# Fourier mixing and a gated feed-forward on one core: column blocks of 512, 512 and 481, with the left 66 tokens of each batch collected in one buffer

## The chip, the core and the metric

The kernel runs on one core of a Trainium2 chip. The engines that matter here are TensorE (PE, matrix multiply; its weight loads are listed as PEld), VectorE (DVE), ScalarE (ACT), GpSimd (POOL) and SyncE (SP), whose queue issues most of the DMAs. Each engine runs its own instructions in order and waits for others by semaphores. The DMAs of all queues run on the core's 16 DMA engines. The metric is the time of one execution on the device, in microseconds (us); lower is better.

## The reference

The input x has 8 batches of 3008 tokens with 256 channels. The reference takes the real part of a two-dimensional Fourier transform over tokens and channels, and sends every token through a feed-forward layer with a ReLU gate.

```python
X = np.fft.fft(x, axis=1)
X = np.fft.fft(X, axis=2)
x = X.real.astype(np.float32).reshape(B * S, D)      # B, S, D = 8, 3008, 256
gate = np.maximum(x @ w_gate, 0.0)                   # w_gate: 256 x 1536
val = x @ w_val
out = (gate * val @ w_out).astype(np.float32)        # w_out: 1536 x 256
```

## The kernel before, in words

**The transform.** The transform of a real signal is symmetric, so the output token k and its mirror S-k are made of the same two parts, a cosine part and a sine part, once added and once subtracted. The kernel folds the input of a batch (POOL, `fold_steps`, lines 102 to 151), multiplies the folded rows with sine and cosine tables on PE (`dft_steps`, L385), and keeps the two parts of 1505 token columns in the tiles `U` and `V`. The channel transform is multiplied into the weights beforehand: `WA` and `WB` are applied to `U` and `V`, and `WM` is the matrix that turns a plus token into its mirror token (minus 2 times `WB`).

**Tiles.** The 1505 columns of a batch are cut into blocks: in batch 0 into four `segments` of 376 or 377, in batches 1 to 7 into three `thirds` of 504, 504 and 497. For every block the kernel goes over the NF = 12 chunks `fi` of 128 of the 1536 hidden channels. One such tile gives `h`, a bf16 tile of 128 hidden channels by two halves, plus and minus, of up to 512 columns each. The minus half is written in reverse order of columns.

**A slot** (`slot`, batches 1 to 7) is one round of the loop over tiles. PE's order in it is: the sine part of the next tile (L689, one matmul), some output steps, the cosine part of the next tile (L696, one matmul), the mirror matmul of the tile before (L575), the value of this tile (L570 and L571, two matmuls), and the rest of the output steps. DVE's order is: the minus product of the tile before (`second`, L597), the plus product of this tile (L597), and the sum for the next tile (`both`, L700). ACT copies the sine part out (L692) and writes a seed into a PSUM bank (`seed`, L684). POOL makes the second of two gates (L701) and, in batches 1 to 5, the folds of the batch after next in between (`run_fold`). Some tiles (every sixth in batch 1, every twelfth in batches 2 to 5) are of an older kind: three gate matmuls in place of the sine and cosine parts, and no L701. The DFT matmuls of the next batch are spread over the first two blocks of a batch, in groups of three (`DFT_EVEN`, `DFT_ODD`); each six of them are followed by two copies on ACT and two sums on DVE (`sums`, L397).

**Output steps** (`out_steps`). When a block's twelve `h` tiles are there, its output is made during the next block. A unit is 128 columns of one half: 12 matmuls (L496), one for each `h` tile, with `h` as the loaded weights and `wo` as the moving operand, 256 columns wide, which add up in a PSUM tile `o`. Two units share a PSUM tile; after them ACT copies it to a tile `os` (L502, four buffers), and SP stores the rows of each unit (L511), every second row of the output. A block of a batch 1 to 7 has eight units, so 96 steps; `per_tile = len(todo_out) // NF` is the number of steps in a slot, eight. A block's `chunks` list says which 128 columns a unit takes, and which rows of them are stored: 128, 120 or 121, once 127; columns at a border between the four segments belong to two units. After the last block, nothing is left to overlap, and its 96 steps run by themselves.

The order of instructions is fixed when the kernel is built; each engine keeps it.

The change touches `thirds`, `segments`, `first_row`, `out_steps`, `half_h`, `second`, `add_h`, `tile_of` and `per_tile`.

Of the kernel before, what the change touches and what calls it, by code (L numbers as in the profile page):

```python
# [11 lines left out]
BF16 = mybir.dt.bfloat16  # L12
# [15 lines left out]
def dram(ap, offset, pattern):  # L28
    return bass.AP(ap.tensor, offset, [list(p) for p in pattern])
# [3 lines left out]
def kernel(  # L33
# [27 lines left out]
    def single(name, shape, dt=F32, pool=const):  # L61
        return pool.tile(shape, dt, name=name, tag=name)
# [6 lines left out]
    wo = single("wo", [128, NF, D], BF16)  # L69
    hp = ctx.enter_context(tc.tile_pool(name="hp", bufs=2 * NF + 2, space=SB))  # L70

    wr = [[None] * 3 for i in range(2)]
    for c in range(3):
        for i in range(2):
            wr[i][c] = hp.tile([128, 2, 512], BF16, name="h", tag="h")
    XD = single("XD", [128, 2, 3, 2, D])
    XG = single("XG", [128, 2, 3, 2, D])
    PQ = single("PQ", [128, 2, 3, 2, D])
# [96 lines left out]
    def iota(dst, pattern, base, mult):  # L175
        nc.gpsimd.iota(dst, pattern=pattern, base=base, channel_multiplier=mult, allow_small_or_imprecise_dtypes=True)
# [41 lines left out]
            load_mirror(0, t, r)  # L218

    def load_w(i, c):  # L220
        nc.gpsimd.dma_start(out=wr[i][c][:], in_=(moe_w_gate, moe_w_val)[i][:, c * 512:(c + 1) * 512].rearrange("(c p) f -> p c f", p=128))
    for c in range(3):
        for i in range(2):
            load_w(i, c)
# [35 lines left out]
    for n, c in enumerate(order):  # L260
        q, m = (single(f"{s}{c}", [128, NJ], pool=st_) for s in "qm")
# [41 lines left out]
    for t in range(3):  # L303
        p, ts = slice(0, ROWS[1][t]), slice(t, t + 1)
# [154 lines left out]
    def new_uv():  # L459
# [2 lines left out]

    thirds = [
# [3 lines left out]
    ]  # L469
    segments = [(s * NJ, NJ, [(0, 0, 128, s, 0), (128, 0, 128, s, 128), (248, 8, 120, s, 256)], None) for s in range(3)]  # L470
    segments.append((3 * NJ, NE, [(0, 1, 127, 3, 0), (128, 0, 128, 3, 127), (249, 7, 121, 3, 255)], (0, 0)))

    def first_row(seg, j, plus):

        if seg == 0:
            return 2 * j + 1 if plus else S - 2 * j - 1
        if seg == 1:
            return H + 2 * j + 1 if plus else H - 2 * j - 1
        if seg == 2:
            return H + 2 * j if plus else H - 2 * j  # L480
        return 2 * j + 2 if plus else S - 2 * j - 2

    def out_steps(b, block, hs):
        c0, n, chunks, zero = block
        units = [(sign, ch) for sign in range(2) for ch in range(len(chunks))]
        steps = []
        for k in range(0, len(units), 2):
            st = {}
            for q in range(2):
                sign, ch = units[k + q]  # L490
                h0 = n - 128 - chunks[ch][0] if sign else chunks[ch][0]
                for f in range(NF):
                    def mm(st=st, q=q, f=f, sign=sign, h0=h0):
                        if "p" not in st:
                            st["p"] = psO.tile([128, 2, D], F32, name="o", tag="o")
                        nc.tensor.matmul(st["p"][:, q, :], lhsT=hs[f][:, sign, h0:h0 + 128], rhs=wo[:, f, :],  # L496
                                         start=(f == 0), stop=(f == NF - 1))
                    steps.append(mm)

            def fin(st=st, k=k):  # L500
                os_ = rp.tile([128, 2, D], F32, name="os", tag="os", bufs=4)
                nc.scalar.copy(os_[:], st["p"][:])  # L502
                for q in range(2):
                    sign, ch = units[k + q]
                    _, p0, cnt, seg, j = chunks[ch]
                    r0 = first_row(seg, j, sign == 0)
                    if seg == 2 and j == 0 and sign == 1:
                        p0, cnt, r0 = p0 + 1, cnt - 1, r0 - 2
                    if sign:
                        p0, r0 = 128 - p0 - cnt, r0 - 2 * (cnt - 1)  # L510
                    nc.sync.dma_start(out=dram(out, (b * S + r0) * D, [[2 * D, cnt], [1, D]]),  # L511
                                      in_=os_[p0:p0 + cnt, q, :])
                    if zero and zero[0] == ch and sign == 0:
                        nc.sync.dma_start(out=dram(out, b * S * D, [[D, 1], [1, D]]), in_=os_[zero[1]:zero[1] + 1, q, :])
# [28 lines left out]
    todo_out, todo_dft, todo_fold = [], [], []  # L543
# [42 lines left out]

    def half_h(st, sign):

        return st["h"][:, 1, st["n"] - 1::-1] if sign else st["h"][:, 0, 0:st["n"]]

    def mult(st, sign, r=None):
        n = st["n"]
        nc.vector.tensor_tensor(half_h(st, sign), (r or st["r"])[:, 0:n], st["v"][:, 0:n], op=ALU.mult)  # L593

    def relu_mult(st, sign):
        n = st["n"]
        nc.vector.scalar_tensor_tensor(half_h(st, sign), in0=st["s"][1 + sign][:, 0:n], scalar=0.0, in1=st["v"][:, 0:n],  # L597
                                       op0=ALU.max, op1=ALU.mult)

    def second(st):  # L600
        (relu_mult if "s" in st else mult)(st, 1)

    def finish(st):
        mirror(st["v"], st, 1)
        second(st)
# [8 lines left out]
        relu(st)  # L614

    def tile_of(block, fi, uvc):
        c0, n = block[:2]
        cols = slice(c0, c0 + n)
        return {"n": n, "fi": fi, "f": slice(fi * 128, (fi + 1) * 128), "us": uvc[0][:, cols], "vs": uvc[1][:, cols], "c": uvc[2][:, cols]}

    def add_h(st, hs):
        st["h"] = hp.tile([128, 2, 512], BF16, name="h", tag="h")
        hs.append(st["h"])

    def single_tile(st, outs, extra=(), last=(), tag="p"):
# [39 lines left out]
    def new_tiles():  # L665
        for b in range(1, B):
            for blk, block in enumerate(thirds):
                for fi in range(NF):
                    st = tile_of(block, fi, uv[b])
                    st["kind"] = "o" if b < 6 and fi % (6 if b < 2 else 12) == 5 else "n"  # L670
                    yield st

# [30 lines left out]
    def slot(cur, mid, nxt, after, outs, fold_us):  # L703
# [20 lines left out]
        if pending is not None:  # L724
            second(pending)
# [16 lines left out]

    uv = {0: (U, V, CB)}
    tiles, ahead = new_tiles(), []

    for b in range(B):
# [4 lines left out]
        for blk, block in enumerate(blocks):  # L751
            hs = []
# [8 lines left out]
            if blk == (0 if b else 2) and b + 1 < B:  # L761
# [94 lines left out]
```

## Time and profile before

| | before |
|---|---|
| time, median of 3 runs | 647.6 us (647.58 to 647.83) |
| span of the profiled execution, first to last instruction | 646.1 us |
| what lies around the span, median less span | 1.5 us |
| granted TensorE clock | 1.000 |
| busy in the span | PE 620.9, PEld 401.6, DVE 543.7, ACT 450.6, POOL 535.5 us |
| output matmuls (L496) | 2304, of 128x256 |
| stores of output rows on SP | 200 |

All lines that follow are of one profiled execution. In a row of the timeline the columns are: start, duration (both in us from the span's start), engine, line of the kernel, operation, the tile written and those read, shape and count; what stands in brackets is idle time of the engine before it, and who ended it. In a row of the windows table the columns are: the stretch, its length, then the busy time of PE, PEld, DVE, ACT and POOL with instruction counts, then the granted clock, the mean busy share of the 16 DMA engines, and GB/s. SPq is SP's queue: a DMA's row there is its issue. Matmuls overlap in the pipeline, so the distance from start to start of two matmuls, not the duration of one, says what it costs. The first two batches differ from the others in their staging; the steady part runs from about 115 us, the first block of batch 1, to 631 us, and the end, output only, from there.

### The profile page before, as it was taken

The numbers are of one execution on the slowest core, as the hardware profiler recorded it, in microseconds if no ns is written. First come the engines' busy times: TensorE is split into PE (matmuls) and PEld (weight loads), VectorE is DVE, ScalarE is ACT, GpSimd is POOL, SyncE is SP. The second block draws the span as 40 slices with busy tenths as digits, with TensorE's granted clock in tenths as the row PEclk, the third lists the DMA queues.
The fourth block names the chain that finished last, engine by engine and source line by source line (L and its number), as shares of the span: only waits on it lengthen the run. The fifth ranks groups of instructions, "written<-read, shape, count | busy, mean of one in ns | idle before, by whom it ended". The sixth has DMA issues, their size and how long they took to land.

```text
span 646.1 us, 12223 instructions
## 1 busy us (share of the span) xinstructions
PE 620.9 (96%) x4160; PEld 401.6 (62%) x4160; DVE 543.7 (84%) x970; ACT 450.6 (70%) x822; POOL 535.5 (83%) x593
## 2 busy tenths in 40 slices
PE   0999999999999999999999999999999999999996
PEld 0356676566666666666666666666666666666665
DVE  8875566887888899898998889988899899999990
ACT  8697666767666776777677677676777767777751
POOL 8589997899999999999899999999876656666660
PEclk9999999999999999999999999999999999999999
DMA  8922544224332433241222422311211111111112
GB/s 227 207 67 64 178 127 137 62 68 145 89 83 63 127 98 90 64 136 58 89 84 78 129 73 82 93 35 49 73 34 49 44 62 49 35 48 49 50 49 79
DMA packets 42438, 55.24 MB, mean 85 GB/s; under 512 B 5153, under 2 KB 32353, under 8 KB 42376
## 3 DMA queue, kind: packets, MB, share of 16 engines
q1 hardware_dynamic: 34552, 39.23, 19.7%
q0 software_dynamic: 7536, 14.72, 9.3%
q8 instruction: 32, 0.52, 0.4%
q10 hardware_dynamic: 288, 0.52, 0.2%
q14 instruction: 30, 0.25, 0.1%
HBM read 32.14 MB, written 24.67 MB: 88 GB/s over the span
## 4 chain that ended last, share of the span: by engine, by line
PE 69%; DVE 12%; POOL 9%; issue 6%; ACT 3%; DMA 0%; DVEq 0%; SPq 0%; ACTq 0%; POOLq 0%
PE o L496 27%; PE v L575 7%; PE v L570 7%; PE v L571 7%; DVE h L597 6%; PE g L689 5%; PE p L696 5%; DVE r L700 5%; POOL r L701 4%; PE d L385 4%; PE p L575 1%; POOL XG L113 1%; POOL PQ L121 1%; POOL XG L102 1%; PE p L571 1%
## 5 line engine op out<-in xcount | busy, mean ns | idle before, releaser
L701 POOL TENSOR_TENSOR r<-r 128x504 f32<-128x504 f32 (+1 forms) x234 | 291.7, 1252 | 73.8 <-DVE r L700 72.3
L496 PE MATMUL o<-wo,h 128*128 128x256 bf16 x2304 | 342.3, 273 | 0.0
L597 DVE SCALAR_TENSOR_TENSOR h<-r,v 128x504 bf16<-128x504 f32 (+1 forms) x468 | 297.3, 673 | 51.1 <-PE v L575 37.8
L496 PEld LDWEIGHTS <-h 128*128 128x128 bf16 x2304 | 225.2, 98 | 114.7 <-issue 2.3
L684 ACT ACTIVATE p<-CB,b 128x504 f32<-128x504 bf16 (+1 forms) x234 | 160.0, 684 | 55.3 <-DVE r L700 52.8
L692 ACT COPY r<-g 128x504 f32<-128x504 f32 (+1 forms) x234 | 135.0, 577 | 58.6 <-PE g L689 54.5
L700 DVE SCALAR_TENSOR_TENSOR r<-r,p 128x504 f32<-128x504 f32 (+1 forms) x234 | 156.7, 670 | 0.6 <-ACT r L692 0.6
L575 PE MATMUL v<-V,WM 128*128 128x504 bf16 (+3 forms) x296 | 108.6, 367 | 1.6 <-DVE h L597 1.0
L570 PE MATMUL v<-U,WA 128*128 128x504 bf16 (+3 forms) x296 | 108.6, 367 | 0.1
L571 PE MATMUL v<-V,WB 128*128 128x504 bf16 (+3 forms) x296 | 108.7, 367 | 0.0
L593 DVE TENSOR_TENSOR h<-r,v 128x376 bf16<-128x376 f32 (+3 forms) x124 | 68.9, 580 | 25.7 <-PE v L575 13.6
L689 PE MATMUL g<-V,WM 128*128 128x504 bf16 (+1 forms) x234 | 87.8, 375 | 0.5 <-ACT r L692 0.3
L696 PE MATMUL p<-U,WA 128*128 128x504 bf16 (+1 forms) x234 | 87.8, 375 | 0.0
L502 ACT COPY os<-o 128x512 f32<-128x512 f32 x96 | 55.7, 580 | 14.5 <-PE o L496 8.1
L570 PEld LDWEIGHTS <-WA 128*128 128x128 bf16 x366 | 35.7, 98 | 38.3 <-issue 8.9
L571 PEld LDWEIGHTS <-WB 128*128 128x128 bf16 x366 | 35.7, 98 | 35.7 <-ACT WB L291 0.7
L102 POOL DMA_INDIRECT XG<-in_x_dram,gidx x48 | 48.8, 1017 | 8.7 <-issue 6.3
L113 POOL TENSOR_TENSOR XG<-XG,XD 128x510 f32<-128x510 f32 x42 | 52.5, 1265 | 0.1
L585 ACT ACTIVATE r<-g 128x504 f32<-128x504 f32 (+3 forms) x48 | 27.3, 569 | 35.0 <-PE g L571 31.8
L585 ACT ACTIVATE r<-p 128x376 f32<-128x376 f32 (+1 forms) x80 | 38.2, 490 | 18.7 <-PE p L575 10.9
L121 POOL TENSOR_TENSOR PQ<-XG 128x510 f32<-128x510 f32 x42 | 45.0, 1091 | 0.0
L575 PEld LDWEIGHTS <-WM 128*128 128x128 bf16 x366 | 35.8, 98 | 11.4 <-issue 0.2
(127 smaller groups left out, 430.4 us busy)
## 6 DMA issues: line engine op xcount, KB each, us to landing
out_dram<-os SPq DMA_DIRECT2D x118, 128.0 KB
XD<-in_x_dram SPq DMA_DIRECT2D x30, 256.0 KB
out_dram<-os SPq DMA_DIRECT2D x62, 120.0 KB
XD<-in_x_dram SPq DMA_DIRECT2D x16, 240.0 KB
CB<-ch SPq DMA_DIRECT2D x7, 376.2 KB
out_dram<-os SPq DMA_DIRECT2D x10, 127.0 KB
XG<-in_x_dram,gidx POOLq DMA_INDIRECT x48
h<-in_moe_w_gate_dram POOLq DMA_DIRECT2D x3, 256.0 KB
```

The source lines that it names most:

```text
L496: nc.tensor.matmul(st["p"][:, q, :], lhsT=hs[f][:, sign, h0:h0 + 128], rhs=wo[:, f, :], start=(f == 0), stop=(f == NF - 1))
L570: nc.tensor.matmul(bank[:, 0:st["n"]], lhsT=WA[i][:, st["f"]], rhs=st["us"], start=True, stop=False)
L571: nc.tensor.matmul(bank[:, 0:st["n"]], lhsT=WB[i][:, st["f"]], rhs=st["vs"], start=False, stop=True)
L575: nc.tensor.matmul(bank[:, 0:st["n"]], lhsT=WM[i][:, st["f"]], rhs=st["vs"], start=False, stop=True, skip_group_check=True)
L593: nc.vector.tensor_tensor(half_h(st, sign), (r or st["r"])[:, 0:n], st["v"][:, 0:n], op=ALU.mult)
L597: nc.vector.scalar_tensor_tensor(half_h(st, sign), in0=st["s"][1 + sign][:, 0:n], scalar=0.0, in1=st["v"][:, 0:n], op0=ALU.max, op1=ALU.mult)
L684: nc.scalar.activation(st["p"][:, 0:st["n"]], st["c"], ACTF.Copy, scale=b2[:, st["fi"]:st["fi"] + 1])
L689: nc.tensor.matmul(st["g"][:, 0:n], lhsT=WM[0][:, st["f"]], rhs=st["vs"], start=True, stop=True)
L692: nc.scalar.copy(q[:, 0:n], st["g"][:, 0:n])
L696: nc.tensor.matmul(st["p"][:, 0:n], lhsT=WA[0][:, st["f"]], rhs=st["us"], start=False, stop=True, skip_group_check=True)
L700: nc.vector.scalar_tensor_tensor(sp[:, 0:n], in0=q[:, 0:n], scalar=-0.5, in1=st["p"][:, 0:n], op0=ALU.mult, op1=ALU.add)
L701: nc.gpsimd.tensor_tensor(sm[:, 0:n], sp[:, 0:n], q[:, 0:n], op=ALU.add)
```

## The change

The three blocks of a batch become 512, 512 and 481 columns wide. The two halves of an `h` tile now stand directly one behind the other, 2n columns, and a unit takes 128 of these 2n columns, across the border of the halves if it falls so. 512 columns make 2 x 512 / 128 = 8 whole units. 481 columns make 962 = 7 x 128 + 66: seven whole units, and 66 columns are left. After the minus product of each tile of such a block, a DMA on SP's queue copies these 66 columns of `h` to `LB`, a buffer of 12 x 256 columns that is filled as a ring over the batches (`keep_rest`). As soon as 128 columns are collected, the block's output gets one more unit that reads them from `LB`; in the last batch the 78 that remain make a unit of 78. `per_tile` is rounded up; blocks with 7 units have 84 steps, 7 in a slot. The segments of batch 0 keep six units each, the last of which overlaps the one before. The rows to store are worked out column by column (`row_of`), and a unit is stored in as many DMAs as it has runs of rows with a distance of two; a border between segments inside a unit cuts a run.

```diff
-            wr[i][c] = hp.tile([128, 2, 512], BF16, name="h", tag="h")
+            wr[i][c] = hp.tile([128, 1024], BF16, name="h", tag="h")[:].rearrange("p (c f) -> p c f", c=2)
...
-    thirds = [
-        (0, 504, [(0, 0, 128, 0, 0), (128, 0, 128, 0, 128), (256, 0, 120, 0, 256), (376, 0, 128, 1, 0)], None),
-        (504, 504, [(0, 0, 128, 1, 128), (128, 0, 120, 1, 256), (248, 0, 128, 2, 0), (376, 0, 128, 2, 128)], None),
-        (1008, 497, [(0, 0, 120, 2, 256), (121, 0, 128, 3, 0), (249, 0, 128, 3, 128), (369, 8, 120, 3, 256)], (0, 120)),
-    ]
+    thirds = [(0, 512), (512, 512), (1024, 481)]
+    segments = [(s * NJ, NJ) for s in range(3)] + [(3 * NJ, NE)]
+    REST = 33
+    LB = single("LB", [128, NF, 256], BF16)
+    left_rows, left_done = [], 0
...
     def out_steps(b, block, hs):
-        c0, n, chunks, zero = block
-        units = [(sign, ch) for sign in range(2) for ch in range(len(chunks))]
+        nonlocal left_done
+        c0, n = block
+        r = [row_of(c0 + i, True) for i in range(n)] + [row_of(c0 + n - 1 - i, False) for i in range(n)]
+        r = [None if v is None else b * S + v for v in r]
+        units, whole = [], n // 64
+        if n < 481:
+            whole = 6
+        for k in range(whole):
+            h0 = min(128 * k, 2 * n - 128)
+            units.append((lambda f, h0=h0: hs[f][:, h0:h0 + 128], [None] * (128 * k - h0) + r[128 * k:h0 + 128]))
+        if n == 481:
+            left_rows.extend(r[128 * whole:])
+            while len(left_rows) - left_done >= 128 or b == B - 1 and left_done < len(left_rows):
+                o = left_done
+                k = min(128, len(left_rows) - o)
+                units.append((lambda f, o=o, k=k: LB[:, f, o % 256:o % 256 + k], left_rows[o:o + k]))
+                left_done += k
...
-                        nc.tensor.matmul(st["p"][:, q, :], lhsT=hs[f][:, sign, h0:h0 + 128], rhs=wo[:, f, :],
+                        nc.tensor.matmul(st["p"][0:m, q, :], lhsT=lhs(f), rhs=wo[:, f, :],
                                          start=(f == 0), stop=(f == NF - 1))
...
+                if len(some[-1][1]) == 128:
+                    nc.scalar.copy(os_[:, 0:len(some)], st["p"][:, 0:len(some)])
+                for q, (_, r) in enumerate(some):
+                    if len(some[-1][1]) < 128:
+                        nc.scalar.copy(os_[0:len(r), q], st["p"][0:len(r), q])
+                    p = 0
+                    while p < len(r):
+                        e = p + 1
+                        while r[p] is not None and e < len(r) and r[e] == r[e - 1] + 2:
+                            e += 1
+                        if r[p] is not None:
+                            nc.sync.dma_start(out=dram(out, r[p] * D, [[2 * D, e - p], [1, D]]), in_=os_[p:e, q, :])
+                        p = e
...
     def half_h(st, sign):
-        return st["h"][:, 1, st["n"] - 1::-1] if sign else st["h"][:, 0, 0:st["n"]]
+        n = st["n"]
+        return st["h"][:, 2 * n - 1:n - 1:-1] if sign else st["h"][:, 0:n]
...
+    def keep_rest(st):
+        o, h0 = 2 * REST * (st["b"] - 1) % 256, 896
+        while h0 < 962:
+            k = min(962 - h0, 256 - o)
+            nc.sync.dma_start(out=LB[:, st["fi"], o:o + k], in_=st["h"][:, h0:h0 + k])
+            o, h0 = 0, h0 + k
...
     def second(st):
         (relu_mult if "s" in st else mult)(st, 1)
+        if st["n"] == 481:
+            keep_rest(st)
...
-            per_tile = len(todo_out) // NF
+            per_tile = -(-len(todo_out) // NF)
```

More of the change, by code (lines that the diff above doesn't have):

```diff
@@ L220, in load_w @@
     def load_w(i, c):
-        nc.gpsimd.dma_start(out=wr[i][c][:], in_=(moe_w_gate, moe_w_val)[i][:, c * 512:(c + 1) * 512].rearrange("(c p) f -> p c f", p=128))
+        nc.gpsimd.dma_start(out=wr[i][c], in_=(moe_w_gate, moe_w_val)[i][:, c * 512:(c + 1) * 512].rearrange("(c p) f -> p c f", p=128))
     for c in range(3):
@@ L460, in new_uv, with row_of @@
         return [up.tile([128, 4 * NJ + 2], BF16, name=n, tag=n) for n in ("U", "V")]
-    thirds = [
[3 rows of a table removed]
-    ]
-    segments = [(s * NJ, NJ, [(0, 0, 128, s, 0), (128, 0, 128, s, 128), (248, 8, 120, s, 256)], None) for s in range(3)]
-    segments.append((3 * NJ, NE, [(0, 1, 127, 3, 0), (128, 0, 128, 3, 127), (249, 7, 121, 3, 255)], (0, 0)))
-    def first_row(seg, j, plus):
+    thirds = [(0, 512), (512, 512), (1024, 481)]
[3 more added lines that the diff above has]
+    left_rows, left_done = [], 0
+    def row_of(col, plus):
+        seg, j = (3, col - 3 * NJ) if col >= 3 * NJ else divmod(col, NJ)
         if seg == 0:
@@ L479, in first_row @@
         if seg == 2:
-            return H + 2 * j if plus else H - 2 * j
-        return 2 * j + 2 if plus else S - 2 * j - 2
+            return H + 2 * j if plus else (H - 2 * j if j else None)
+        return 2 * j if plus else (S - 2 * j if j else None)
     def out_steps(b, block, hs):
-        c0, n, chunks, zero = block
-        units = [(sign, ch) for sign in range(2) for ch in range(len(chunks))]
+        nonlocal left_done
[15 more added lines that the diff above has]
+                left_done += k
         steps = []
@@ L488, in out_steps, with mm @@
             st = {}
-            for q in range(2):
-                sign, ch = units[k + q]
-                h0 = n - 128 - chunks[ch][0] if sign else chunks[ch][0]
+            some = units[k:k + 2]
+            for q, (lhs, r) in enumerate(some):
                 for f in range(NF):
-                    def mm(st=st, q=q, f=f, sign=sign, h0=h0):
+                    def mm(st=st, q=q, f=f, lhs=lhs, m=len(r)):
                         if "p" not in st:
                             st["p"] = psO.tile([128, 2, D], F32, name="o", tag="o")
-                        nc.tensor.matmul(st["p"][:, q, :], lhsT=hs[f][:, sign, h0:h0 + 128], rhs=wo[:, f, :],
+                        nc.tensor.matmul(st["p"][0:m, q, :], lhsT=lhs(f), rhs=wo[:, f, :],
@@ L497, in mm, with fin @@
                                          start=(f == 0), stop=(f == NF - 1))
                     steps.append(mm)
-            def fin(st=st, k=k):
+            def fin(st=st, some=some):
                 os_ = rp.tile([128, 2, D], F32, name="os", tag="os", bufs=4)
[L502 to L514, printed above, removed]
+                if len(some[-1][1]) == 128:
[11 more added lines that the diff above has]
+                        p = e
@@ L616, in tile_of @@
     def tile_of(block, fi, uvc):
-        c0, n = block[:2]
+        c0, n = block
         cols = slice(c0, c0 + n)
@@ L621, in add_h @@
     def add_h(st, hs):
-        st["h"] = hp.tile([128, 2, 512], BF16, name="h", tag="h")
+        st["h"] = hp.tile([128, 1024], BF16, name="h", tag="h")
         hs.append(st["h"])
@@ L669, in new_tiles @@
                     st = tile_of(block, fi, uv[b])
+                    st["b"] = b
                     st["kind"] = "o" if b < 6 and fi % (6 if b < 2 else 12) == 5 else "n"
```

## The prediction

> **What bounds the kernel now.** I read the page's busy times first, then the timeline of a slot in the steady part, then that of a slot with fewer output steps, then the DMA table by short windows around single stores and at the end. The page says that PE decides:
>
> ```profile
> span 646.1 us, 12223 instructions
> PE 620.9 (96%) x4160; PEld 401.6 (62%) x4160; DVE 543.7 (84%) x970; ACT 450.6 (70%) x822; POOL 535.5 (83%) x593
> ```
>
> The timeline shows a steady slot (batch 4, last block, 497 columns), from one `value` matmul of L571 to the next:
>
> ```profile
> 403.65 0.37 PE L571 MATMUL v<-V,WB 128*128 128x497 bf16 x1
> 403.71 1.26 DVE L597 SCALAR_TENSOR_TENSOR h<-r,v 128x497 bf16<-128x497 f32 x2 [0.15 <-PE v L575]
> ...
> 404.40 0.71 PE L496 MATMUL o<-wo,h 128*128 128x256 bf16 x5
> ...
> 405.57 0.37 PE L571 MATMUL v<-V,WB 128*128 128x497 bf16 x1
> ```
>
> 405.57 - 403.65 = 1.92 us. Matmuls overlap: their starts stand 0.109 us apart at 256 columns and 0.21 at 504, so five wide ones and eight output steps make 5 x 0.21 + 8 x 0.109 = 1.92: PE has no gap. At 504 columns the trace repeats 1.936. DVE needs three operations a slot; two of them take 1.26 of which the last lasts 0.67, so they follow each other every 0.59, and three need 1.77 of 1.94: the second bound is only 0.17 below. Where a slot has six output steps (batch 1, first block), that second bound shows:
>
> ```profile
> 116.01 0.38 PE L575 MATMUL v<-V,WM 128*128 128x504 bf16 x1
> ...
> 116.44 0.38 PE L571 MATMUL v<-V,WB 128*128 128x504 bf16 x1
> ...
> 116.50 1.27 DVE L597 SCALAR_TENSOR_TENSOR h<-r,v 128x504 bf16<-128x504 f32 x2 [0.55 <-PE v L575]
> ...
> 117.82 0.37 PE L575 MATMUL v<-V,WM 128*128 128x504 bf16 x1
> 117.82 0.10 PEld L570 LDWEIGHTS <-WA 128*128 128x128 bf16 x1 [0.20 <-issue]
> ...
> 118.24 0.37 PE L571 MATMUL v<-V,WB 128*128 128x504 bf16 x1
> ```
>
> PE would need 1.936 - 2 x 0.109 = 1.72; the slot takes 1.80, since the mirror matmul at 117.82 waits for the two DVE products (116.50 + 1.27 = 117.77), which waited for the mirror matmul before. That loop is a floor under every slot.
>
> The third thing is the stores. The page counts ten of 127 rows:
>
> ```profile
> out_dram<-os SPq DMA_DIRECT2D x10, 127.0 KB
> ```
>
> One is issued at 563.44. The windows after it, and those at the kernel's end (last two columns: busy share of the 16 DMA engines, GB/s):
>
> ```profile
> 567.00:568.00 1.00, 1.00 (x8) 0.63 (x7) 0.99 (x2) 0.58 (x1) 0.39 (x1) 1.00 0.07 26
> 568.00:569.00 1.00, 1.00 (x9) 0.70 (x8) 0.93 (x2) 0.97 (x2) 0.93 (x1) 1.00 0.07 25
> 569.00:570.00 1.00, 1.00 (x9) 0.62 (x7) 0.93 (x2) 0.74 (x3) 0.33 (x1) 1.00 0.07 24
> ```
>
> ```profile
> 642.00:643.00 1.00, 0.00 (x0) 0.00 (x0) 0.00 (x0) 0.42 (x1) 0.00 (x0) 1.00 0.00 0
> 643.00:644.00 1.00, 0.00 (x0) 0.00 (x0) 0.00 (x0) 0.00 (x0) 0.00 (x0) 1.00 0.55 169
> 644.00:645.00 1.00, 0.00 (x0) 0.00 (x0) 0.00 (x0) 0.00 (x0) 0.00 (x0) 1.00 0.29 85
> 645.00:646.00 1.00, 0.00 (x0) 0.00 (x0) 0.00 (x0) 0.00 (x0) 0.00 (x0) 0.91 0.00 0
> ```
>
> A share of 0.07 is one engine of 16: the 127 rows run one after the other at 24 to 26 GB/s, 42.5 ns for a row of 1 KB. By the completion events in the trace such a store lands 7.2 us after its issue at best (median of the ten 7.6), one of 128 rows in 1.7 to 1.8 and one of 120 in 1.9 to 2.0 at quiet times. Today's last two stores (128 and 120 rows, issued at 642.45 and 642.85) have landed at 644.83; the span ends 1.3 later.
>
> **PE's part.** Batches 1 to 7 make 24 output units each, 168; after, 23 each and 4 units of collected rows, 165. Three units x 12 matmuls = 36 fewer, which the instruction order confirms (72 PE rows less, a load and a matmul each). At 0.109 that is 3.9 us. They fall in three places, the first blocks of batches 2, 4 and 6, where per_tile goes from 8 to 7. Wider and narrower blocks cancel: 24 slots a batch gain 8 columns and 12 lose 16, at 5 matmuls x 0.42 ns (0.109 us for 256) both ways.
>
> Not all of the 3.9 arrives. A slot with 512 columns and 7 steps needs 1.936 + 8 x 5 x 0.42 ns - 0.109 = 1.84 on PE. The loop above grows by 8 columns in one matmul and two products, 8 x (0.42 + 1.0 + 1.0) ns = 0.02, to 1.83 (1.0 ns is DVE's step: 0.46 us back to back at 376 columns, 0.59 at 504). So the slot just fits, but the DFT's four sums a block (L397, every 0.26 us when back to back) lose their cover: 1.94 - 1.77 = 0.17 a slot today, 0.05 after. Batch 1's first block prices this: from its first L571 matmul at 114.24 to the next block's at 138.54 it takes 24.30. PE alone would take the 25.43 of batch 2's first block, less 24 x 0.109, plus one matmul of 0.21 for its second tile of the old kind: 23.03. Of the 1.27 over, eight slots x 0.08 = 0.7 is the floor, and 0.57 is sums. With 7 steps I take 0.5 a block, 1.5 in all; the bounds are 0 and 4 x 0.26 x 3 = 3.1. POOL adds a little: in batch 2's first block its result (L701) is ready only 0.03 and 0.5 us before DVE takes it at two tiles, and the block would be 1.1 shorter. Bounds 0 and 0.6, I take 0.2, as DVE's lead of some 0.4 covers most. Batch 1, already at the floor and behind POOL, gets wider tiles in 24 slots and loses 0 to 0.3; I take 0.1. Sum: 3.9 - 1.5 - 0.2 - 0.1 = 2.1 us gained.
>
> **The copies of the left 66 columns.** 96 DMAs (seven times 12, one batch split in two) of 128 x 132 B, put on SP's queue behind `second`, and 48 more stores; at 0.25 to 0.43 us of issue each some 50 us on a queue that spent 421 us waiting for `os L502`. Queued behind a copy are only stores: `os` has four buffers and is reused some 23 us later. The row loads for XD are issued in first blocks, where only tile 11's copy stands. The matmuls that read LB come 84 steps, over 9 us, after that copy's issue, also at the end, against about 2 us for a small store: cost 0; without that cover it would be 2 us once. 48 LB weight loads wait for a DMA; today's weight loads with a satisfied wait (L689 behind a DMA) start on the usual 0.109 beat, so 0. The product that overwrites a copied `h` comes 26 tiles, 50 us, later: 0.
>
> **The end.** Here the change costs. The row runs are cut at segment borders, and in the last block of a batch the stores have 104+24, 128, 128, 97+31, 128, 128, 89+38 rows, then the collected rows, in batch 7 12+66. In the trace the completion events of a store number 16 for 128 rows, 15 and one at once for 120, 11 and one for 121, one and one for 127 and for 1: the number of engines is the largest divisor of the row count up to 16. 97, 31 and 89 have none, so each runs on one engine, and by the trace on the same one: the 127 rows issued at 630.93 land at 638.13, and the four stores behind them (128, 120, 1 and 128 rows) are complete only after that, at 638.5 to 639.2, 3.9 to 7.2 us from their issue.
> The Trainium skill's page "DMA: Bandwidth & Descriptors", section "Why a DMA increments its semaphore by 16 and not by 1", states the same: the largest k up to 16 that divides the outer sizes, on the lowest-numbered engines. The counts above agree for 1, 120, 121, 127 and 128 rows; no run shows 97, 31 or 89. By that rule the sum is the one that follows; by the quiet 120-row stores the end would cost 0.4.
>
> The second pair of the last block is copied at 636.60 in today's frame, so its 97 rows are issued at about 637.6. From there the first engine has 97 + 31 + 8 + 8 + 89 + 19 (38 rows on two) + 1 + 6 (66 on eleven) = 259 rows x 42.5 ns = 11.0 us. A 127-row store has 7.2 - 5.4 = 1.8 besides its rows. 637.6 + 1.8 + 11.0 = 650.4, against 644.8: 5.6 late. The 1.8 holds some receipt that a chain may not repeat, so I take 5.4. Bounds: 0.4 if these stores spread (only two more issues of some 0.35 at the end, less one smaller copy), 6.3 if each single-engine store brings the 0.3 us hiccup that the packets of the one at 631 show. In mid-kernel the same stores are late by as much and nobody waits.
>
> **The sum.** Span 646.1 - 2.1 + 5.4 = 649.4. The median of the timed runs, 647.6, is 1.5 above this execution's span; so 650.9.
>
> **Rivals.** (a) Faster: the stores of 97, 31 and 89 rows spread over engines like those of 120. Then 647.6 - 2.1 + 0.4 = 645.9. For it: none of these counts is in the trace; against: ten 127-row stores and the event counts. It decides when the last 89 rows land within 3 us of their issue. 0.10. (b) The whole of PE's 3.9 arrives since DVE absorbs the sums in the slots that also hold DFT matmuls (2.42 long), and the end costs 4.6 (a start 0.6 earlier, quick receipt): 647.6 - 3.9 + 4.6 = 648.3. 0.10. (c) Slots with seven steps fall to DVE and POOL altogether: gain 3.9 - 3.1 = 0.8 or less, end 5.4 or more, 652.2 to 652.9. 0.12. (d) That fewer matmuls are not made: excluded by the instruction order.
>
> **How the numbers follow.** The forecast has 0.68, rival (c) 0.12 on the same side, (b) 0.10, (a) 0.10. A change of 0.2%, 1.3 us, is about what a measurement can tell here: under 646.3 is faster, over 648.9 slower. Slower 0.68 + 0.12 = 0.80, same 0.10 from (b), faster 0.10 from (a). The range runs from (b), 648.2, to (c), 652.9, and leaves out (a) and the edges of the others.
>
> **What would show it.** Right: PE's last matmul some 2 us earlier than 641.5, and after it about 8 us with nothing busy but a DMA share near 0.07; the first blocks of batches 2, 4 and 6 at about 24.7 instead of 25.4; no wait of PE for a copy into LB. Wrong: a DMA share of 0.3 or more in the last microseconds and an end within 4 us of PE's last matmul (then (a)); those blocks at 24.3 (then (b)) or unshortened (then (c)); a wait of PE for an LB copy.

## The result and the profile after

| | before | after |
|---|---|---|
| median of four runs each, us | 647.72 (647.58 to 647.95) | 652.09 (651.80 to 652.47) |
| span of the profiled execution, us | 646.1 | 650.1 |
| PE's last matmul ends, us | 641.76 | 639.34 |
| last store has landed, us | 644.83 | 648.80 |

The changed kernel takes 1.0069 times as long (95% interval 1.0054 to 1.0083): 4.4 us slower. PE is done 2.4 us earlier, and the end, from there to the last row in memory, has grown from 3.07 to 9.46 us.

In the changed kernel the output matmul is L511 (L496 before), the copies of its result are L518 and L521, the stores L528, the products L620 (L597 before; L609 in tiles of the older kind), the mirror matmul L590, the value matmuls L585 and L586, the sum `both` L726, POOL's second gate L727, and the copy into `LB` L615. The line numbers of the experiments are some more by the lines that were added.

The first lines of the page of the changed kernel. PE's busy time reads 5.3 us lower, but 47 matmuls have no record in this trace (4124 weight loads, 4077 matmuls). In the run below that copies into `LC`, where all 4124 are recorded, it reads 618.8, which is 2.1 below before. The other engines have kept their busy time:

```profile
span 650.1 us, 12382 instructions
PE 615.6 (95%) x4077; PEld 398.0 (61%) x4124; DVE 543.5 (84%) x970; ACT 450.6 (69%) x823; POOL 535.4 (82%) x593
```

The windows of the changed kernel after PE's last matmul, against those shown of before:

```profile
641.00:642.00 1.00, 0.00 (x0) 0.00 (x0) 0.00 (x0) 0.00 (x0) 0.00 (x0) 0.67 0.07 25
642.00:643.00 1.00, 0.00 (x0) 0.00 (x0) 0.00 (x0) 0.00 (x0) 0.00 (x0) 0.50 0.11 36
643.00:644.00 1.00, 0.00 (x0) 0.00 (x0) 0.00 (x0) 0.00 (x0) 0.00 (x0) 0.50 0.27 71
644.00:645.00 1.00, 0.00 (x0) 0.00 (x0) 0.00 (x0) 0.00 (x0) 0.00 (x0) 0.50 0.13 44
645.00:646.00 1.00, 0.00 (x0) 0.00 (x0) 0.00 (x0) 0.00 (x0) 0.00 (x0) 0.50 0.07 25
646.00:647.00 1.00, 0.00 (x0) 0.00 (x0) 0.00 (x0) 0.00 (x0) 0.00 (x0) 0.50 0.07 25
647.00:648.00 1.00, 0.00 (x0) 0.00 (x0) 0.00 (x0) 0.00 (x0) 0.00 (x0) 0.50 0.07 24
648.00:649.00 1.00, 0.00 (x0) 0.00 (x0) 0.00 (x0) 0.00 (x0) 0.00 (x0) 0.50 0.03 9
```

No engine computes in any of them, and in four of the eight the DMA share is 0.07 at 24 to 25 GB/s: one engine of 16 with rows of 1 KB, one after the other. The granted clock falls to 0.50 here, with no matmul to run; one engine moved no more, 24 to 26 GB/s, in the kernel before at 567 to 570 us, where the clock was 1.00. SP's waits in the last 16 us of the changed kernel (what waited, for what; us in total, times, longest) say the same: the wait at the kernel's end (L877) stands 5.4 us for a store.

```profile
SPq L877 <- DMA out_dram<-os: 5.4, 1, 5.4
```

The stores at the end by their issue and their landing (completion events of the trace):

| rows | issued at | landed at | completion events |
|---|---|---|---|
| 97 | 635.20 | 641.32 | 2 |
| 31 | 635.52 | 642.63 | 2 |
| 128 | 637.42 | 642.98 | 16 |
| 128 | 637.82 | 643.32 | 16 |
| 89 | 639.82 | 647.64 | 2 |
| 38 | 640.12 | 648.44 | 3 |
| 12 | 641.91 | 648.62 | 13 |
| 66 | 642.82 | 648.80 | 12 |

Each event comes from one engine, except that where there are fewer than 16, one comes at once: 97, 31 and 89 rows ran on one engine, 38 on two. The Trainium skill's page "DMA: Bandwidth & Descriptors", section "Why a DMA increments its semaphore by 16 and not by 1", says that the number of engines is the largest one up to 16 that divides the count, and that the lowest-numbered engines are taken. The events agree for each of these counts. The stores of 128, 12 and 66 rows, spread as they were, had all but one of their engines done early (those of 128 rows by 640.05 and 641.08, of 12 and 66 rows by 644.37 and 644.63) and landed only when the last engine, the one that also had the 97, 31 and 89 rows, was through.

The steady part has changed where the steps fell from 8 to 7 a slot. The first blocks of batches 2, 4 and 6 went from 25.43, 25.43 and 25.26 to 24.94, 24.94 and 24.85 us. A slot of the changed kernel, batch 6, first block, in which one of the DFT's sums stands ahead of the products on DVE (timeline):

```profile
495.14 0.38 PE L586 MATMUL v<-V,WB 128*128 128x512 bf16 x1
...
495.15 0.34 DVE L397 SCALAR_TENSOR_TENSOR V<-es,d 128x188 bf16<-128x188 f32 x1
...
495.41 1.28 DVE L620 SCALAR_TENSOR_TENSOR h<-r,v 128x512 bf16<-128x512 f32 x2
...
496.74 0.38 PE L590 MATMUL v<-V,WM 128*128 128x512 bf16 x1
496.74 0.10 PEld L585 LDWEIGHTS <-WA 128*128 128x128 bf16 x1 [0.31 <-issue]
...
497.17 0.38 PE L586 MATMUL v<-V,WB 128*128 128x512 bf16 x1
```

The products start 0.27 us after the value matmul because of the sum (0.06 in the slot of before that the prediction shows, which has no sum) and end at 496.69; the mirror matmul needs the bank that they read and starts at 496.74, after 0.31 us without a weight load. The slot lasts 497.17 - 495.14 = 2.03 us, where slots with neither a sum nor DFT matmuls take 1.84. It is the same loop that batch 1 showed before.

Of the copies into `LB` nothing is felt. The trace's answer on that tile lists the reading matmuls, and under the idle time before them and who waited it has no entry:

```profile
L615 SPq DMA_DIRECT2D LB<-h x96: 464/471/1568, 168.2 to 629.7; - x96
L511 PE MATMUL o<-wo,LB x48: 272/273/273, 283.8 to 639.1; 128*128 128x256 bf16 x36, 128*78 128x256 bf16 x12
```

### The profile page after: what moved, and what is told of

Read it like the earlier page. It is cut to its first block, busy times and chain, and to the rows that moved or that the text cites. A ratio compares the mean times of both kernels' runs of the same rounds, so it can differ in the third digit from the quotient of the medians.

```text
span 650.1 us, 12382 instructions
## 1 busy us (share of the span) xinstructions
PE 615.6 (95%) x4077; PEld 398.0 (61%) x4124; DVE 543.5 (84%) x970; ACT 450.6 (69%) x823; POOL 535.4 (82%) x593
## 4 chain that ended last, share of the span: by engine, by line
PE 86%; DVE 6%; POOL 3%; issue 2%; ACT 1%; DVEq 0%; ACTq 0%; POOLq 0%
PE o L511 35%; PE v L586 9%; PE v L590 9%; PE v L585 7%; PE g L715 7%; PE p L722 7%; PE d L385 4%; POOL r L727 1%; DVE h L620 1%; PE p L590 1%; PE p L586 1%; PE p L585 1%; DVE h L609 1%; PE d L443 1%; ACT r L600 1%
## 5 line engine op out<-in xcount | busy, mean ns | idle before, releaser
L727 POOL TENSOR_TENSOR r<-r 128x512 f32<-128x512 f32 (+1 forms) x234 | 291.7, 1253 | 71.5 <-DVE r L726 70.0
L620 DVE SCALAR_TENSOR_TENSOR h<-r,v 128x512 bf16<-128x512 f32 (+1 forms) x468 | 297.2, 673 | 49.2 <-PE v L590 35.4
L511 PE MATMUL o<-wo,h 128*128 128x256 bf16 x2220 | 331.7, 272 | 0.0
L511 PEld LDWEIGHTS <-h 128*128 128x128 bf16 x2220 | 216.8, 98 | 112.2 <-issue 2.3
L710 ACT ACTIVATE p<-CB,b 128x512 f32<-128x512 bf16 (+1 forms) x234 | 160.1, 684 | 55.8 <-DVE r L726 54.7
L718 ACT COPY r<-g 128x512 f32<-128x512 f32 (+1 forms) x234 | 135.3, 578 | 56.5 <-PE g L715 49.1
L726 DVE SCALAR_TENSOR_TENSOR r<-r,p 128x512 f32<-128x512 f32 (+1 forms) x234 | 156.7, 669 | 0.6 <-ACT r L718 0.6
L590 PE MATMUL v<-V,WM 128*128 128x512 bf16 (+3 forms) x296 | 108.6, 367 | 2.2 <-DVE h L620 0.9
L586 PE MATMUL v<-V,WB 128*128 128x512 bf16 (+3 forms) x296 | 108.6, 367 | 2.0
L585 PE MATMUL v<-U,WA 128*128 128x512 bf16 (+3 forms) x258 | 94.2, 365 | 0.1
L609 DVE TENSOR_TENSOR h<-r,v 128x376 bf16<-128x376 f32 (+3 forms) x124 | 68.9, 581 | 25.7 <-PE v L590 13.6
L715 PE MATMUL g<-V,WM 128*128 128x512 bf16 (+1 forms) x234 | 87.8, 375 | 0.5 <-ACT r L718 0.3
L722 PE MATMUL p<-U,WA 128*128 128x512 bf16 (+1 forms) x227 | 85.1, 375 | 0.0
L518 ACT COPY os<-o 128x512 f32<-128x512 f32 x95 | 54.5, 573 | 12.4 <-PE o L511 8.1
L585 PEld LDWEIGHTS <-WA 128*128 128x128 bf16 x366 | 35.7, 98 | 40.0 <-issue 11.3
L586 PEld LDWEIGHTS <-WB 128*128 128x128 bf16 x366 | 35.7, 98 | 35.7 <-ACT WB L291 0.7
L102 POOL DMA_INDIRECT XG<-in_x_dram,gidx x48 | 48.8, 1018 | 8.6 <-issue 6.0
L590 PEld LDWEIGHTS <-WM 128*128 128x128 bf16 x366 | 35.8, 98 | 11.5 <-issue 0.2
```

The costliest lines, as they stand in the source:

```text
L511: nc.tensor.matmul(st["p"][0:m, q, :], lhsT=lhs(f), rhs=wo[:, f, :], start=(f == 0), stop=(f == NF - 1))
L585: nc.tensor.matmul(bank[:, 0:st["n"]], lhsT=WA[i][:, st["f"]], rhs=st["us"], start=True, stop=False)
L586: nc.tensor.matmul(bank[:, 0:st["n"]], lhsT=WB[i][:, st["f"]], rhs=st["vs"], start=False, stop=True)
L590: nc.tensor.matmul(bank[:, 0:st["n"]], lhsT=WM[i][:, st["f"]], rhs=st["vs"], start=False, stop=True, skip_group_check=True)
L710: nc.scalar.activation(st["p"][:, 0:st["n"]], st["c"], ACTF.Copy, scale=b2[:, st["fi"]:st["fi"] + 1])
L715: nc.tensor.matmul(st["g"][:, 0:n], lhsT=WM[0][:, st["f"]], rhs=st["vs"], start=True, stop=True)
```

## The experiments

The kernel before, run beside them on the same chip each time, took 647.65 to 647.66 us. All ratios are against it, with 95% intervals. One thing limits comparisons of single profiles: the first block of batch 1 starts between 113.91 and 114.47 us in profiles of kernels whose batch 0 is the same, so some 0.5 us of a difference between two spans may come from there.

**Stores spread.** The changed kernel, with every run of rows whose count has no divisor from 8 to 16 cut in two so that the first part has one (97 into 96 and 1, 31 into 30 and 1, 89 into 88 and 1, 38 into 36 and 2).

```diff
+    def parts(n):
+        even = lambda m: m < 8 or any(m % k == 0 for k in range(8, 17))
+        cut = next(c for c in range(n) if even(n - c))
+        return [n - cut] + ([cut] if cut else [])
...
-                            nc.sync.dma_start(out=dram(out, r[p] * D, [[2 * D, e - p], [1, D]]), in_=os_[p:e, q, :])
+                            for cnt in (parts(e - p)):
+                                nc.sync.dma_start(out=dram(out, r[p] * D, [[2 * D, cnt], [1, D]]), in_=os_[p:p + cnt, q, :])
+                                p += cnt
```

> The changed kernel, with every run of rows whose count has no divisor from 8 to 16 cut in two so that the larger piece has one (97 into 96 and 1, 31 into 30 and 1, 89 into 88 and 1, 38 into 36 and 2); all else as changed. If the end is long because those stores run on one DMA engine, PE ends as in the changed kernel (about 639.3 in the span) and the last store, issued at about 641.6 after six issues of 0.35 us, lands at 643.5 instead of 648.8: span 644.8, time 646.5 to 647.0, 0.7 to 1.2 us below the kernel before. If the end is long because there are more stores in it, a half-size unit of collected rows and two small copies, then four more stores make it longer still: 652 to 654.

Measured: 646.68 us (646.32 to 646.93), ratio 0.9981 (0.9972 to 0.999). The 88 rows land 1.72 us after their issue, where the 89 took 7.82, and the last row is in memory 3.84 us after PE's end instead of 9.46. The windows of the end of this kernel:

```profile
641.00:642.00 1.00, 0.00 (x0) 0.00 (x0) 0.00 (x0) 0.00 (x0) 0.00 (x0) 1.00 0.43 120
642.00:643.00 1.00, 0.00 (x0) 0.00 (x0) 0.00 (x0) 0.00 (x0) 0.00 (x0) 0.89 0.16 43
643.00:644.00 1.00, 0.00 (x0) 0.00 (x0) 0.00 (x0) 0.00 (x0) 0.00 (x0) 0.50 0.17 47
```

The stretch at 0.07 is gone. The odd rows, one or two in a store, cost the kernel 5.4 us and turned a small gain into a loss.

**Stores spread in the last block alone.** The same, but runs are cut only in the last block of the last batch; in all others the stores of 97, 31 and 89 rows stay on one engine.

```diff
-                            for cnt in (parts(e - p)):
+                            for cnt in (parts(e - p) if (b, n) == (B - 1, 481) else [e - p]):
```

> The same cut, but only in the stores of the very last block; in all blocks before it the stores of 97, 31, 89, 38 and so on stay whole on one or two engines. If these cost nothing in mid-kernel, as the forecast had it, the time is that of e1_spread within 0.3 us. If they hold up PE there (os buffers that come free late, SP blocked, XD rows behind them on the same engine), part of the loss of the changed kernel stays and it is 0.5 us or more above e1_spread.

Measured: 646.18 us (646.08 to 646.53), ratio 0.9973 (0.9963 to 0.9984). From the first block of batch 1 to the last tile the two kernels take 513.26 and 513.24 us. So the one-engine stores in the middle of the kernel cost nothing that these profiles show; the kernel pays for them only where nothing is left to run beside them. The median is 0.50 below the first experiment's, more than the 0.3 that was expected; in the two profiles 0.26 of that is the start of batch 1, and the rest was not followed. This version is the base of most of what follows.

**The same row counts in the kernel before.** In its last block, a store of 120 rows is cut into 97 and 23, and one of 128 into 89, 38 and 1.

```diff
+                    cuts = {(2, 1): (97, 23), (6, 0): (89, 38, 1)}.get((k, q)) if (b, n) == (B - 1, 497) else None
+                    for c in cuts or (cnt,):
+                        nc.sync.dma_start(out=dram(out, (b * S + r0) * D, [[2 * D, c], [1, D]]),
+                                          in_=os_[p0:p0 + c, q, :])
+                        p0, r0 = p0 + c, r0 + 2 * c
```

> The kernel before, with its old blocks and no collecting, where in the last block of the last batch one store of 120 rows is cut into 97 and 23 and one of 128 into 89, 38 and 1. By the one-engine theory the first engine gets 97 + 23 + 8 + 8 + 89 + 19 + 1 + 8 = 253 rows from about 638.8 on, 42.5 ns each, plus the 0.8 us of hiccups that the changed kernel showed: the last store lands at about 650.7 instead of 644.8, time 653.3 to 653.9, 5.7 to 6.2 us above the kernel before. If the number of stores and the collected unit make the end long, three more stores add 0.7 to 1.2 us: 648.4 to 648.9.

Measured: 654.12 us (653.71 to 655.84), ratio 1.0104 (1.0088 to 1.0119), a little above the expected range. PE ends at 641.64 (641.76 in the kernel before), and then the windows show the picture of the changed kernel:

```profile
643.00:644.00 1.00, 0.00 (x0) 0.00 (x0) 0.00 (x0) 0.00 (x0) 0.00 (x0) 1.00 0.08 27
...
647.00:648.00 1.00, 0.00 (x0) 0.00 (x0) 0.00 (x0) 0.00 (x0) 0.00 (x0) 0.50 0.07 25
648.00:649.00 1.00, 0.00 (x0) 0.00 (x0) 0.00 (x0) 0.00 (x0) 0.00 (x0) 0.50 0.07 25
649.00:650.00 1.00, 0.00 (x0) 0.00 (x0) 0.00 (x0) 0.00 (x0) 0.00 (x0) 0.50 0.07 24
```

The 89 rows are issued at 642.33 and land at 649.71, and a store of 120 rows behind them at 650.92. So row counts by themselves, without any other part of the change, make the loss; with the first experiment this shows it from both sides.

**No collection.** The second experiment's kernel without `LB`: the 66 left columns are made by an eighth unit of the block, which overlaps the seventh. The blocks of 512, 512 and 481 and the spread end stay.

```diff
+        if n == 481:
+            whole = 8
...
-        if n == 481:
+        if n == 0:
             left_rows.extend(r[128 * whole:])
...
-        if st["n"] == 481:
-            keep_rest(st)
```

> e2_spread_last without the collecting: blocks of 512, 512 and 481, the left 66 columns of each batch as an eighth unit that overlaps the seventh, 36 matmuls more, no copies, eight steps in every slot. The forecast's step on PE says that collecting brings not 3.9 but some 2.0 us, since the first blocks of batches 2, 4 and 6 go back from 24.94, 24.94 and 24.85 to 25.65, 25.65 and 25.46; the end has one store and one copy less, 0.3: 647.6 to 648.1. If the 36 matmuls cost their full 0.109 us each, 649.5 to 650.1.

Measured: 648.92 us (648.72 to 649.40), ratio 1.0019 (1.0009 to 1.0028), 2.74 more than with collection. That lies between the two expectations. PE ends at 642.22 against 639.59, of which 0.3 is the start of batch 1. So the 36 matmuls that collecting saves bring 2.3 us and not the 3.9 that they cost one by one, and the new block widths alone bring nothing.

**Copies twice.** The second experiment's kernel, each copy into `LB` issued a second time to the same place.

```diff
-            nc.sync.dma_start(out=LB[:, st["fi"], o:o + k], in_=st["h"][:, h0:h0 + k])
+            for again in range(2):
+                nc.sync.dma_start(out=LB[:, st["fi"], o:o + k], in_=st["h"][:, h0:h0 + k])
```

> e2_spread_last with every copy of the left 66 columns into LB issued twice (96 more DMAs of 128 x 132 B on SP's queue). By the forecast the copies lie beside other work: 646.0 to 646.5, as e2_spread_last. If they hold up SP's queue so that PE waits, or slow PE's or DVE's access to SBUF, the first copying has cost about as much as the second: 0.5 us or more above.

Measured: 676.57 us (675.54 to 678.31), ratio 1.0452 (1.0436 to 1.0469): 30 us more than without the second copies, a miss. The waits of this kernel (what waited, for what; us in total, times, longest):

```profile
SPq L623 <- DMA LB<-h: 127.1, 95, 3.7
...
PEld L516 <- DMA LB<-h: 23.3, 7, 4.5
PE o L516 <- DMA LB<-h: 20.8, 7, 4.3
...
ACT os L523 <- DMA out_dram<-os: 14.5, 4, 7.5
```

The second copy writes where the first does, so it waits on SP's queue until the first has landed. Everything behind it on SP, copies and stores, then runs late: PE waits for copies, and ACT for `os` buffers. Most of the loss lies in the first block of batch 5, which makes a collected unit (44.07 us, 25.65 in the changed kernel; one slot of 16.35), and at the end. Not all of it is waiting: after PE had stood for copies, the granted clock was 0.50 from 436.9 to 457.4 us, and matmuls of 512 columns started 0.43 us apart in place of 0.21. PE ran without a gap from 452.8 to 457.4 at that pace, so some 2.3 us of the loss there are matmuls at half the clock, by an estimate from these numbers. The run had added waits, and not copies alone, so the next one takes the wait away.

**Copies twice, to another place.** The second copy goes into a buffer `LC` that nothing reads.

```diff
+    LC = single("LC", [128, NF, 66], BF16)
...
             nc.sync.dma_start(out=LB[:, st["fi"], o:o + k], in_=st["h"][:, h0:h0 + k])
+            nc.sync.dma_start(out=LC[:, st["fi"], h0 - 896:h0 - 896 + k], in_=st["h"][:, h0:h0 + k])
```

> e2_spread_last (646.18) with every copy into LB made a second time into another buffer that nothing reads, so that, unlike in e6_copies_twice, the second copy doesn't wait on SP's queue for the first to land. If the copies themselves cost nothing where they lie, 646.0 to 646.6, and the 30 us of e6_copies_twice were SP's waiting (127 us in all) and nothing else. If the bytes or the issues cost, part of the 30 us comes back: 648 or more.

Measured: 646.67 us (646.60 to 646.89), ratio 0.998 (0.9971 to 0.999). The interval overlaps that of one copy (0.9963 to 0.9984). By the trace nearly all of the 0.49 between the medians lies in two slots, of batches 6 and 7, that are 0.22 us longer and in which DVE starts its products 0.4 us late; why was not followed. No matmul waits for `LB`. So 96 copies more cost 0 to half a microsecond, and nothing suggests that those of the change cost more; but the run before shows what they live on, the slack of SP's queue.

**Steps moved off the sums' slots.** If sums lengthen slots that have room for more matmuls, output steps can be moved there from the DFT's slots. The first experiment's kernel, with the 84 steps of these blocks dealt by a list, two more to each slot with a sum and two fewer to each with DFT matmuls.

```diff
+    HEAD = (4, 3, 4, 3, 4, 5, 5, 3, 4, 3, 4, 5)
+    TAIL = (2, 3, 2, 3, 4, 4, 2, 3, 2, 3, 4, 5)
...
+            if share:
+                upto = {3: share[0] * 3 // 5, 5: share[0], 8: sum(share)}[part]
```

> e1_spread, and in the three blocks with 84 output steps two steps each are moved from the four slots that hold DFT matmuls into the four slots where DVE makes the sums (head and tail of a slot given one by one, in sum again 84). If the 0.6 to 0.7 us lost in each of these blocks are sums of DVE without PE work beside them, the four long slots (2.03 to 2.05 us) stay as they are, the DFT slots fall from 2.33 to 2.11, and each block takes 24.1 to 24.3 instead of 24.9: 1.5 to 2.1 us below e1_spread. If POOL or the loop of mirror matmul and products sets the pace of the whole block, moving steps changes nothing: within 0.4 us of e1_spread.

Measured: 646.57 us (646.22 to 647.12), ratio 0.998 (0.9971 to 0.9989): nothing against the first experiment, a miss. DFT slots fell from 2.33 to 2.11 us and the sums' slots hardly grew, to 2.06. But the last slot of batch 6's block took 2.57 in place of 2.05. Its timeline:

```profile
510.90 0.71 PE L516 MATMUL o<-wo,h 128*128 128x256 bf16 x5 [0.23 <-ACT os L523]
510.90 0.42 PEld L516 LDWEIGHTS <-h 128*128 128x128 bf16 x4 [0.52 <-issue]
```

The list had let a pair of units end one slot later than it used to, so PE stood 0.52 us for the copy out of their PSUM tile: the edit's own fault.

**The same with a better list**, on the second experiment's kernel, six steps moved and the pair's end kept where it was.

```diff
-    HEAD = (4, 3, 4, 3, 4, 5, 5, 3, 4, 3, 4, 5)
-    TAIL = (2, 3, 2, 3, 4, 4, 2, 3, 2, 3, 4, 5)
+    HEAD = (4, 3, 4, 3, 4, 5, 5, 3, 4, 4, 4, 5)
+    TAIL = (2, 3, 2, 3, 4, 4, 2, 3, 3, 3, 4, 3)
```

> e2_spread_last (646.18), and the steps moved as in e4_spread_rebalanced but mended: there the copy of the third output pair came one slot late and the last slot of the block took 2.57 us instead of 2.05, which gave the gain back. Here two steps each leave three of the DFT slots, go to three of the sum slots, and the third pair ends where it did. If the sums lacked PE work beside them, the three DFT slots fall from 2.33 to 2.11 and the sum slots stay at 2.03 to 2.06: the first blocks of batches 2, 4 and 6 take 24.3 to 24.5, 24.3 to 24.4 and 24.2 to 24.3 instead of 24.94, 24.94 and 24.85, time 644.4 to 644.9. If POOL sets the pace in batches 2 and 4 (where e4_spread_rebalanced showed DFT slots of 2.45 and 2.18 in place of 2.11), those two give up to 0.35 us less, time up to 645.4. If neither, no change: 646.2.

Measured: 645.12 us (645.00 to 645.49), ratio 0.9961 (0.9947 to 0.9975). Batch 6's block falls by 0.62 as expected, to 24.23, near the 24.15 that PE alone needs (25.46 for a block of eight steps, less 12 x 0.109). Batch 4's falls by 0.34: one of the sums lies beside a tile of the older kind, which has one DVE operation less, so that slot had lost nothing. So the time lies in the second of the two ranges that were expected. Batch 2's block falls by 0.08. There a slot still takes 2.44, in which DVE waits for POOL (timeline of that slot):

```profile
192.63 3.73 POOL L734 TENSOR_TENSOR r<-r 128x512 f32<-128x512 f32 x3
...
193.94 1.28 DVE L627 SCALAR_TENSOR_TENSOR h<-r,v 128x512 bf16<-128x512 f32 x2 [0.58 <-POOL r L734]
```

**The order of the last units.** The kernel just shown, with the last block's units in another order, so that the whole ones of 128 rows are stored last and the cut ones earlier.

```diff
+        if (b, n) == (B - 1, 481):
+            units = [units[k] for k in (0, 1, 3, 6, 2, 7, 4, 5)]
```

> e4b_rebalanced, and the last block's units are output in the order 0, 1, 3, 6, 2, collected, 4, 5, so that the two units that each need one store of 128 rows come last. The last store then lands about 3.1 us after PE's end, as in the kernel before, and not 3.8 as in e2_spread_last: 0.7 to 0.9 us below e4b_rebalanced, 643.6 to 644.2, about 0.995 of the kernel before. If what is left at the end is the receipt of any last store and not their number, no change against e4b_rebalanced.

Measured: 644.07 us (644.06 to 644.14), ratio 0.9944 (0.993 to 0.9957), as expected; the best version here, 3.6 us below the kernel before and 8.0 below the change as it was made. Two windows of its end: the last rows go out over many engines at once, at 242 GB/s in place of 25, and then nothing is left.

```profile
640.00:641.00 1.00, 0.00 (x0) 0.00 (x0) 0.00 (x0) 0.00 (x0) 0.00 (x0) 0.98 0.71 242
641.00:642.00 1.00, 0.00 (x0) 0.00 (x0) 0.00 (x0) 0.00 (x0) 0.00 (x0) 0.50 0.00 0
```

**POOL lighter.** The best version with fewer folds on POOL in the blocks of 84 steps (0.7 us a slot in place of 0.9) and more in the others (0.95), to free batch 2's slot.

```diff
-                    pending = slot(cur, *ahead, per_tile, 1.1 if b == 1 else .9, shares and shares[fi])
+                    pending = slot(cur, *ahead, per_tile, 1.1 if b == 1 else .7 if shares else .95, shares and shares[fi])
```

> e5_best (644.07) with POOL's fold work of batches 2 to 5 paced otherwise: 0.7 us of it a slot in the blocks with 84 steps and 0.95 in the others, where it was 0.9 everywhere. If POOL is what keeps the first blocks of batches 2 and 4 at 24.86 and 24.60 while batch 6, which has no folds, reaches 24.24, they fall to 24.4 to 24.6 and 24.4 to 24.5, time 643.4 to 643.8; the second blocks must take the work and may give back up to 0.3. If it is not POOL, 644.07 within 0.2.

Measured: 644.27 us (643.99 to 644.71), ratio 0.9945 (0.9931 to 0.9958): no gain, a miss. The blocks of batches 2 and 4 keep their 24.86 and 24.59, and the slot of 2.44 stays. The edit did not reach that slot: it is the third of its block, and up to its end POOL runs the same instructions in the same order in both kernels, two gathers of input rows (L102) of 1.02 to 1.04 us each among the second gates. The pace only changes what follows. So whether POOL with less to do there would free the slot stays open.

## Why the prediction came out right

Predicted 650.9 us (648.2 to 652.9), measured 652.1; the sign and the mechanism were right, and the step that missed most is a size. By its steps:

- **PE's 3.9 us, less what does not arrive.** Predicted gain 2.1. PE's last matmul is 2.42 earlier; 0.30 of it was there at the start of batch 1, within what that start varies by, which leaves 2.12 for the part that the prediction summed. The run without collection gives 2.3. That 2.1 is met so closely is in part luck: the sums took 0.4 more than was allowed for them, and the 0.3 set aside for POOL and batch 1 did not come. The three blocks took 24.94, 24.94 and 24.85 and not the 24.7 named as a sign; that figure left out that they are 8 columns wider, 0.2 a block (25.65 in place of 25.43 with eight steps), which the narrower third block of a batch gives back.
- **The sums' cover.** Taken at 1.5, bounds 0 and 3.1; measured against what PE alone needs (24.34, 24.34 and 24.15, from the same blocks with eight steps, 25.65, 25.65 and 25.46, less 12 x 0.109) the three blocks lose 0.60 + 0.60 + 0.70 = 1.9, in the slots with a sum, as argued. Moving steps into those slots took 0.62 back in batch 6, so there it is shown and not only argued; in batches 2 and 4 it took back 0.08 and 0.34.
- **POOL and batch 1.** Taken at 0.2 and 0.1. In batch 2 no POOL loss showed beside the sums': it lost no more than batch 6, which has no folds. The wait for POOL came out only once the block had been shortened further. Batch 1's three blocks took 75.36 together in place of 75.42, so nothing was lost there.
- **The copies.** Taken at 0; no wait of PE for `LB`, and doubled copies cost at most half a microsecond. The cover that the prediction named, the distance to the reading steps on a queue with slack, is what the run with doubled waits took away: then it cost 30 us.
- **The end, the mis-sized term.** Taken at 5.4 with 6.3 as upper bound; measured 9.46 - 3.07 = 6.4. The chain on the first engine ran as worked out: in the long stretches its rows started 42.4 ns apart. The step that fell short is the hiccups: the prediction put them in the bound alone, and of its "0.3 us hiccup" two came, packets of 0.36 and 0.33 us at 637.07 and 643.37. Beyond a row's own time they are together 0.6 of the 1.0 that was missed. Most of the rest lies in the store of 89 rows: it landed 4.32 after the 128 rows ahead of it (643.32 to 647.64), 0.54 more than 89 x 42.5 ns, and one of the two packets is only 0.28 of that; why was not followed. The median missed by 1.2: 1.0 from this, -0.3 from the early start, and 0.5 since median less span was 2.0, not 1.5.
- **Rivals.** (a), spread stores, would have given 645.9; the first two experiments made that case by hand, 646.7 and 646.2. (b), all of the 3.9: no, 24.9 and not 24.3 in those blocks. (c), nearly nothing of it: no, though the sums took a quarter more than the forecast gave them.

## What to carry to other kernels

Look at the row counts of stores that nothing runs behind: a count whose only divisor up to 16 is 1 went through one DMA engine here, and cutting off the one or two odd rows brought 5.4 us of 652. When work is taken off the bounding engine, look in the profile for a slot that already has less of it, for the second bound shows there, and deal the remaining work towards the slots where the other engine is late. A copy that rides on a queue's slack costs little until something on that queue waits.

## What the runs showed of the hardware that was not expected

- One engine takes rows of 1 KB at 24 to 26 GB/s here. The Trainium skill's page "DMA: Bandwidth & Descriptors", section "Specifications", has about 27 GiB/s for an engine, 29 GB/s; for such rows the measurement is lower, and it decides.
- In this program a DMA that writes over the target of the DMA before it is issued only when that has landed, and all behind it on the queue stands too: 127.1 us in 95 waits, 1.3 us each, for copies of 128 x 132 bytes.
- Behind a store on one engine the next issue on SP took longer: over the changed kernel 0.57 to 3.59 us for 38 rows behind 89, where the 36 rows of the first experiment, behind stores on many engines and one of a single row, took 0.30 each time.
- The stores of 97, 31 and 89 rows in the middle of the kernel, each on one engine, cost nothing that the two profiles with 513.26 and 513.24 us could show.
